# Another cost model and a search in the planner that orders the engines, and other copies in the first head

## The chip, the cores and the metric

The kernel runs on one core of one Trainium2 chip. The metric is the time of one execution on the device in microseconds (us), the median of several runs. Smaller is better.

## The reference

```python
# attention: 2 batches, 8 heads, 768 tokens, 64 values per head
q_bits = (einsum('bhsd,dk->bhsk', q, proj) > 0)        # 6 sign bits of each query; k_bits alike
mask   = q_bucket[:, :, :, None] == k_bucket[:, :, None, :]
scores = where(mask, q @ k.T / sqrt(64), -1e9)
attn   = exp(scores - max(scores)); attn /= sum(attn) + 1e-9
x      = attn @ v                                      # rearranged to 1536 tokens x 512
# first MoE layer, 512 -> 1024 -> 1024 -> 512
x = ((x @ w1) * (x @ w2)) @ w3 @ w_out
# second one, 512 -> 1536 -> 512
out = (sigmoid(x @ w_gate) * (x @ w_val)) @ w_out2
```

The weights come as float64. The kernel keeps them as 64-bit words, converts each 128 x 512 block on the chip, and does the products in float32 halves: an operand is split into a high and a low part, and three matmuls (high-high, high-low, low-high) stand for one product.

## The kernel before

The work has two stages. The first holds the attention, the product of `w3` with `w_out` (`wacc`), and the first MoE layer for the first 512 tokens (`p`, `y`). The second is the function `moe`: 16 tiles of the first layer for the other 1024 tokens and 36 tiles of the second layer. Each of these 52 tiles has 36 matmuls of 512 columns in line 703 (tiles `pa`, `pb`, `m`).

The attention goes over 16 heads with six steps each, a step being 128 queries. A step has four score matmuls of 384 columns (lines 473 and 476), a maximum on VectorE (`sm`, line 482, VectorE is DVE in the profile), an exponential on ScalarE (`e`, line 492, ACT), six 128 x 128 transposes on TensorE (`tp`, line 525, PE), evictions of the transposes by ScalarE and VectorE (`pt`, lines 528 and 530) and six matmuls of 256 columns with the values (`av`, line 543). Each head also has eight hash matmuls of 384 columns (`gps`, lines 393 and 396), with a sign on ScalarE (`sg`) between them. From the second head on, GpSimd (POOL) prepares queries and keys (lines 409 to 411). The first head is made in `first_head` with its own copies: ScalarE rounds the queries and keys to `aq` (line 448), VectorE subtracts this to get `bq` (line 449), GpSimd casts the swapped half twice (`bk`, `ak`, line 453), and ScalarE copies the other half of `bk` (from line 454 on, shown in the trace under the copy helper at line 282). The matrix `pq`, which the hash matmuls read, is written by VectorE at lines 826 and 827 from `pq_raw`, for which ScalarE's queue issues two transfers (lines 434 and 435). The activation table is loaded by an exponential at line 437 that writes into `thr`, the tile that VectorE fills at line 828.

A weight block is loaded into a tile `st` (line 326) and converted by `decode` in six instructions: two on ScalarE (`da`, `dr`, lines 342 and 343), two on GpSimd (`dr`, `da`, lines 344 and 345), a shift on VectorE (`da`, line 346) and a joining operation on VectorE (line 351). 40 of the 76 blocks are converted in the first 345 us.

What sets the order of the first stage is the planner `order_engines`. It is called once, after the first stage's instructions are emitted and before `moe`. It plays the instructions through time with a price for each (`cost`), a delay from engine to engine (`step`), the rings of buffers (`blocked`) and one queue for all transfers. Whenever an engine is free it takes the ready instruction with the lowest `bass_priority`. The order that comes out is pinned, engine by engine, by dependencies that cost no wait between engines. The prices decide nothing on the chip but this order. `moe` is not planned by it.

Of the kernel before, what the change touches and what calls it, by code (L numbers as in the profile page):

```python
# [45 lines left out]
def order_engines(tc):  # L46
# [11 lines left out]
    def count(x):  # L58
        n = 1
        for _, c in list(x.ap)[1:]:  # L60
            n *= c
        return n

    def region(x):

        b = getattr(x, "bass_ap", None)
        if b is None or b.tensor.name not in rings:
            return None
        ap = [list(p) for p in b.ap]
        es = mybir.dt.size(b.dtype)  # L70
        p0, f0 = divmod(b.offset, ap[0][0]) if ap[0][0] else (0, b.offset)
        f1 = f0 + sum((c - 1) * abs(st) for st, c in ap[1:]) + 1
        return b.tensor.name, p0, p0 + ap[0][1], f0 * es, f1 * es

    def cost(k):
        i, e, op = ins[k], eng[k], type(ins[k]).__name__
        rd = [x for x in i.ins if hasattr(x, "ap")]
        n = max([count(i.outs[0])] + [count(x) for x in rd[:1]])
        banks = [x for x in rd + [i.outs[0]] if (region(x) or ("",))[0] in rings and rings[region(x)[0]][0][0] in ("psT", "psS")]
        if e == "PE":  # L80
            passes = 1 if "float32r" in str(rd[0].dtype) else 2 if n == 128 else 4
            return n / 2.4 * passes + (16 if passes == 1 else -12 if passes == 2 else 4)
        if e == "Activation":
            return 971 if n == 768 and banks else 50 + n * (0.836 if banks else 1.0)
        if e == "Pool":
            if op == "InstTensorTensor":
                return 40 + n * 2.4 if n < 768 else 2200
            return 100 + n * 1.15
        if e == "DVE":
            if op == "InstCustomDveAnt":  # L90
                return 720
# [12 lines left out]
    wrote, read, first, uses = {}, {}, {}, {}  # L104
    over = lambda a, b: a[1] < b[2] and b[1] < a[2] and a[3] < b[4] and b[3] < a[4]
    inside = lambda a, b: b[1] <= a[1] and a[2] <= b[2] and b[3] <= a[3] and a[4] <= b[4]
    for k, i in enumerate(ins):
# [26 lines left out]
    left = [len(deps[k]) + len(starts[k]) for k in range(N)]  # L134
# [5 lines left out]
    queue, opens, held, pools = {}, {}, {}, {}  # L140
    for t in sorted(first, key=first.get):
        queue.setdefault(rings[t][0], []).append(t)
        opens.setdefault(first[t], []).append(t)
        pools[rings[t][0][0]] = pools.get(rings[t][0][0], 0) + 1
        for k in uses[t]:
            held.setdefault(k, []).append(t)
    slots = {g: max(rings[t][1] for t in q) for g, q in queue.items()}
    taken = dict.fromkeys(queue, 0)
    todo = {t: len(u) for t, u in uses.items()}

    def blocked(k):
        for t in opens.get(k, ()):
            g = rings[t][0]
            if slots[g] <= 0 or queue[g][taken[g]] != t:
                return g
            if g[0] == "mw" and pools.get("wtmp"):
                return "wtmp"
        return None

    events, ready, waiting = [], {e: [] for e in ranks}, {}  # L160
    at, free, order = [0.0] * N, dict.fromkeys(ranks, 0.0), {e: [] for e in ranks}
    tick = itertools.count()
    dma = 0.0

    def wake(g):
        for k in waiting.pop(g, ()):
            heapq.heappush(ready[eng[k]], (ins[k].bass_priority, k))

    def post(t, what, x):
        heapq.heappush(events, (t, next(tick), what, x))  # L170

    for k in range(N):
        if not left[k]:
            post(0.0, "ready", k)
    while events:
        now = events[0][0]
        while events and events[0][0] <= now:
            _, _, what, x = heapq.heappop(events)
            if what == "ready":
                heapq.heappush(ready[eng[x]], (ins[x].bass_priority, x))  # L180
            elif what == "slot":
                g = rings[x][0]
                slots[g] += 1
                pools[g[0]] -= 1
                wake(g)
                if not pools[g[0]]:
                    wake(g[0])
            elif what == "end":
                for u in ends[x]:
                    left[u] -= 1  # L190
                    at[u] = max(at[u], now + step.get((eng[x], eng[u]), 60))
                    if not left[u]:
                        post(at[u], "ready", u)
                for t in held.get(x, ()):
                    todo[t] -= 1
                    if not todo[t]:
                        post(now + 200, "slot", t)
        again = True
        while again:
            again = False  # L200
            for e in ranks:
                while free[e] <= now and ready[e]:
                    _, k = heapq.heappop(ready[e])
                    g = blocked(k)
                    if g is not None:
                        waiting.setdefault(g, []).append(k)
                        continue
                    for t in opens.get(k, ()):
                        g = rings[t][0]
                        slots[g] -= 1  # L210
                        taken[g] += 1
                        if slots[g] > 0 and waiting.get(g):
                            wake(g)
                            again = True
                    order[e].append(k)
                    for u in begins[k]:
                        left[u] -= 1
                        at[u] = max(at[u], now)
                        if not left[u]:
                            post(at[u], "ready", u)  # L220
                    free[e] = done = now + cost(k)
                    if type(ins[k]).__name__.startswith("InstDMA"):
                        n = count(ins[k].outs[0]) * list(ins[k].outs[0].ap)[0][1] * mybir.dt.size(ins[k].outs[0].dtype)
                        dma = max(now + 1900, dma) + n / 300
                        done = dma + 900
                    post(done, "end", k)
                    post(free[e], "free", k)
# [8 lines left out]
def lsh_attention_moe_moe2_kernel(  # L236
# [57 lines left out]
    pq_raw = cst.tile([P, NB], F32, name="pq_raw")  # L294
# [3 lines left out]
    nthr = cst.tile([P, 1], F32, name="nthr")  # L298
    zb = cst.tile([P, 1], F32, name="zb")
# [129 lines left out]
    def first_head():  # L429
# [525 lines left out]
```

## Time and profile before

| | us |
|---|---|
| median of 3 runs | 812.64 (812.19 to 812.66) |
| the profiled execution's own time | 809.7 |
| its span, first to last instruction | 807.5 |
| TensorE busy | 783.1 (97%) |
| ScalarE busy | 512.4 (63%) |
| VectorE busy | 471.0 (58%) |
| GpSimd busy | 437.0 (54%) |

Times in the trace are microseconds from the start of the span unless marked ns. A busy share of TensorE near 100% doesn't say that it streams at its full rate: its instructions overlap and their ends are modelled, so the spacing of matmuls is the better measure. The chain of work goes back from the last instruction to what released it, step by step, and shows what the time hung on.

### The profile page before, as it was taken

Reading aid. Unit: us, or ns where it says so; the run is one execution under the profiler, and the core shown is the slowest. Engines: PE = TensorE matmul, PEld = TensorE weight load, DVE = VectorE, ACT = ScalarE, POOL = GpSimd, SP = SyncE. Lnnn points to the kernel's source line nnn. Section 1 sums busy time; section 2 is a strip of 40 time slices with the busy share of each in tenths; the row PEclk is TensorE's granted clock in tenths of the full one; section 3 lists DMA queues with packets and bytes.
Section 4 is the critical chain, followed back from the end, with each engine's and each line's share of the span. In section 5 each row is a group of like instructions: output and inputs, shape, how many; then the busy total and the mean of one; then the engine's idle time right before and its main releaser. Section 6 shows DMA issues by size and latency. Waiting matters only on the chain.

```text
span 807.5 us, 11531 instructions
## 1 busy us (share of the span) xinstructions
PE 783.1 (97%) x4016; PEld 657.3 (81%) x4016; DVE 471.0 (58%) x721; ACT 512.4 (63%) x946; POOL 437.0 (54%) x460
## 2 busy tenths in 40 slices
PE   5899999999999999999999999999999999999998
PEld 4787788888888888988888888888888888888886
DVE  5999997775989799773553535655422222222222
ACT  5999997785989888783465556767434333343332
POOL 6778885675576565286355556777523233332320
PEclk9999999999999999999999999999999999999999
DMA  8767676544456574130022123343001000010001
GB/s 263 200 180 184 170 209 170 141 110 109 108 148 167 131 178 118 39 113 0 27 79 78 53 79 105 124 137 105 0 1 53 0 1 1 0 53 1 0 1 52
DMA packets 28584, 74.44 MB, mean 92 GB/s; under 512 B 6128, under 2 KB 8432, under 8 KB 28528
## 3 DMA queue, kind: packets, MB, share of 16 engines
q1 hardware_dynamic: 28368, 73.73, 32.5%
q8 instruction: 31, 0.51, 0.3%
q14 instruction: 25, 0.20, 0.1%
q10 hardware_dynamic: 160, 0.00, 0.0%
HBM read 52.83 MB, written 3.19 MB: 69 GB/s over the span
## 4 chain that ended last, share of the span: by engine, by line
PE 82%; DVE 9%; ACT 3%; POOL 2%; issue 2%; DMA 0%; ACTq 0%; SPq 0%; DVEq 0%; POOLq 0%
PE m L703 18%; PE pa L703 18%; PE pb L703 18%; PE av L543 6%; PE tp L525 5%; PE p L703 5%; PE wacc L598 4%; PE y L703 3%; PE s L476 3%; PE s L473 3%; DVE pt L530 2%; DVE sm L482 2%; PE gps L393 1%; DVE w3f L351 1%; DVE da L346 1%
## 5 line engine op out<-in xcount | busy, mean ns | idle before, releaser
L743 DVE TENSOR_TENSOR pb<-pb,a 128x512 f32<-128x512 f32 x52 | 36.3, 699 | 178.0 <-PE pb L703 173.2
L697 POOL TENSOR_TENSOR wal<-xall,wah 128x512 fp32r<-128x512 f32 x36 | 47.6, 1323 | 107.0 <-ACT wah L282 107.0
L525 PE MATMUL tp<-idf,e 128*128 128x128 f32 x576 | 99.0, 274 | 2.8 <-DVE pt L530 1.5
L482 DVE TENSOR_REDUCE sm<-s 128x1 f32<-128x768 f32 x96 | 90.7, 947 | 17.6 <-PE s L476 17.4
L530 DVE TENSOR_TENSOR pt<-tp,pt 128x512 fp32r<-128x512 f32 x144 | 94.6, 680 | 9.5 <-ACT pt L528 8.7
L703 PE MATMUL pa<-x,wah 128*128 128x512 f32 x320 | 99.8, 391 | 0.0
L703 PE MATMUL pb<-x,wbh 128*128 128x512 f32 x320 | 98.6, 389 | 0.0
L492 ACT ACTIVATE e<-s,sm 128x768 f32<-128x768 f32 x96 | 86.8, 907 | 14.6 <-DVE sm L482 14.4
L344 POOL TENSOR_SCALAR dr<-st 128x512 bf16<-128x512 f32 x76 | 73.8, 981 | 40.8 <-issue 20.8
L528 ACT ACTIVATE pt<-tp 128x512 fp32r<-128x512 f32 x144 | 82.7, 601 | 10.7 <-PE tp L525 9.1
L525 PEld LDWEIGHTS tp<-idf,e 128*128 128x128 f32 x576 | 70.6, 140 | 13.9 <-DVE pt L530 4.3
L543 PE MATMUL av<-pt,spv 128*128 128x256 f32 x576 | 78.9, 286 | 2.8 <-DVE pt L530 2.6
L543 PEld LDWEIGHTS av<-pt,spv 128*128 128x128 f32 x576 | 73.0, 190 | 7.6 <-DVE pt L530 5.7
L703 PEld LDWEIGHTS pa<-x,wah 128*128 128x128 f32 x320 | 60.1, 188 | 13.6
L703 PEld LDWEIGHTS pb<-x,wbh 128*128 128x128 f32 x320 | 60.1, 188 | 12.6
L473 PE MATMUL s<-bk,bq 128*128 128x384 f32 x192 | 61.6, 370 | 4.6 <-ACT e L492 4.5
L598 PE MATMUL wacc<-wo,t 128*128 128x512 f32 x192 | 65.7, 414 | 0.2 <-POOL wo L593 0.2
L345 POOL TENSOR_SCALAR da<-da 128x512 f32<-128x512 f32 x76 | 48.8, 647 | 26.1 <-ACT da L342 22.5
L703 PE MATMUL pa<-x,wal 128*128 128x512 f32 x160 | 62.9, 393 | 0.0
L703 PE MATMUL pb<-x,wbl 128*128 128x512 f32 x160 | 62.3, 389 | 0.0
L476 PE MATMUL s<-ak,aq 128*128 128x384 f32 x192 | 60.3, 368 | 0.3 <-ACT aq L461 0.3
L343 ACT ACTIVATE dr<-st 128x512 int16<-128x512 uint32 x76 | 60.1, 790 | 0.0
(146 smaller groups left out, 1822.1 us busy)
## 6 DMA issues: line engine op xcount, KB each, us to landing
st<-in_moe_w_dram SPq DMA_DIRECT2D x32, 512.0 KB, 4.8
st<-in_moe_w_out_dram SPq DMA_DIRECT2D x20, 512.0 KB, 4.2
st<-in_moe_w_gate_dram SPq DMA_DIRECT2D x12, 512.0 KB, 3.3
st<-in_moe_w_val_dram SPq DMA_DIRECT2D x12, 512.0 KB, 3.2
qk<-in_qk_dram SPq DMA_DIRECT2D x15, 384.0 KB, 4.1
rawv<-in_v_dram SPq DMA_DIRECT2D x16, 192.0 KB, 2.5
rr<-row SPq DMA_DIRECT2D x16, 192.0 KB, 4.1
out_dram<-o SPq DMA_DIRECT2D x12, 256.0 KB, 2.0
```

The costliest lines, as they stand in the source:

```text
L343: act.activation(out=r.bitcast(I16)[:, 0::2], in_=lw, func=AF.Copy, scale=2.0 ** -29)
L344: pool.tensor_scalar(out=r.bitcast(BF16)[:, 1::2], in0=f(hw), scalar1=0.0, scalar2=1.0, op0=ALU.mult, op1=ALU.mult)
L473: pe.matmul(s[:, half, :HS], lhsT=m["bq"][:, qs], rhs=m["bk"][:, ks], start=True, stop=False)
L476: pe.matmul(s[:, half, :HS], lhsT=m["aq"][:, qs], rhs=m["ak"][:, ks], start=False, stop=True)
L482: dve.tensor_reduce(out=b, in_=s[:, :, :HS], op=ALU.max, axis=AX.XY, negate=True)
L492: act.activation(out=e.rearrange("p (a c) -> p a c", a=2), in_=s[:, :, :HS], func=AF.Exp, bias=sm, scale=1.0, accum_out=su_t[h][:, t:t + 1],)
L525: pe.transpose(ps[:, i * P:(i + 1) * P], e_t[g - g % 2 + a][:, c * P:(c + 1) * P], idf)
L528: act.activation(out=dh, in_=src, func=AF.Copy)
L530: dve.tensor_tensor(out=d, in0=src, in1=f(dh), op=ALU.subtract)
L543: pe.matmul(acc[:w.shape[1], :2 * P].rearrange("p (a t) -> p a t", a=2), lhsT=w, rhs=r[:, :, c], start=(c == 0 and i == 0), stop=(c == NT ...
L598: pe.matmul(acc, lhsT=t3[x][:, j], rhs=wo[y][:, j], start=(j == 0 and n == 0), stop=(j == NF1 - 1 and n == 2))
L703: mm = pe.matmul(ps, lhsT=lhs[x], rhs=rhs[y], start=start and n == 0, stop=stop and n == 2)
```

## The change

The planner's function `cost` gets other prices, and marks the instructions of GpSimd and those instructions of VectorE that have at least 128 columns and touch no PSUM. In the plan, a marked instruction of one of the two engines begins only when the last marked one of the other has ended (`lock`). TensorE's matmuls cost double in the plan while `slow` holds, which follows the share of TensorE's time in use. Matmuls of one engine into one PSUM tile keep their program order (`last`). The whole plan is a function `plan(prio)`. It is called once with the priorities as they are, then 400 times with one to eight of them shifted by 50 to 400 from a fixed seed. A trial is kept where the planned end is no later. This happens when the kernel is built; nothing of it runs on the chip.

In the first head, `pq_raw` is loaded once, to 64 partitions, and read for both halves of `pq`. The activation that loads the table writes into a tile of its own, `warm`. Of the copies of the first head's keys, the lower half of `bk` goes from GpSimd to ScalarE, the upper half from ScalarE to VectorE, and `ak` stays on GpSimd.

```diff
+    port = [False] * N
     def cost(k):
...
+        if op.startswith("InstDMA"):
+            return 500
         if e == "PE":
             passes = 1 if "float32r" in str(rd[0].dtype) else 2 if n == 128 else 4
             return n / 2.4 * passes + (16 if passes == 1 else -12 if passes == 2 else 4)
         if e == "Activation":
-            return 971 if n == 768 and banks else 50 + n * (0.836 if banks else 1.0)
+            if banks:
+                return {768: 878, 512: 478, 256: 405}.get(n, 470)
+            return 40 + n + (96 if es == 2 else 0)
         if e == "Pool":
+            port[k] = True
             if op == "InstTensorTensor":
-                return 40 + n * 2.4 if n < 768 else 2200
-            return 100 + n * 1.15
+                return 30 + n * (2.35 if n < 768 else 2.8)
+            return 140 if n < 128 else 715 if es == 2 else 560 if n > 384 else 450
         if e == "DVE":
-            if op == "InstCustomDveAnt":
-                return 720
-            if op in ("InstTensorTensor", "InstTensorReduce") or (op == "InstTensorScalarPtr" and len(rd) > 1 and count(rd[1]) > 8):
-                return 69 + n * (1.04 if banks else 1.4)
-            return 585 if op == "InstTensorScalarPtr" and n == 384 else 69 + n * 0.6
-        return 600
+            two = op in ("InstTensorTensor", "InstCustomDveAnt") or (op == "InstTensorScalarPtr" and len(rd) > 1 and count(rd[1]) > 8)
+            if op == "InstTensorReduce":
+                return 867
+            port[k] = not banks and n >= 128
+            if two and n >= 512:
+                return 600
+            if two:
+                return 85 + n * 1.17 if banks else 60 + n * 1.1
+            return 589 if banks else 60 + n * 0.55
+        return 500
...
+        for w in W:
+            if rings[w[0]][0][0] in ("psT", "psS"):
+                starts[k].update(last.get((e, w[0]), ()))
+                last[e, w[0]] = {k}
...
+    def plan(prio):
...
+                        if port[k]:
+                            begin = max(now, lock["Pool" if e == "DVE" else "DVE"])
+                            lock[e] = begin + c
+                        free[e] = done = begin + c
...
+        return max(free.values()), order
+
+    prio = [i.bass_priority for i in ins]
+    best, order = plan(prio)
+    rng = random.Random(1)
+    for _ in range(400):
+        trial = list(prio)
+        for _ in range(rng.choice((1, 1, 2, 4, 8))):
+            trial[rng.randrange(N)] += rng.choice((-400, -200, -100, -50, 50, 100, 200, 400))
+        span, o = plan(trial)
+        if span <= best:
+            best, order, prio = span, o, trial
...
-    pq_raw = cst.tile([P, NB], F32, name="pq_raw")
+    pq_raw = cst.tile([D, NB], F32, name="pq_raw")
...
+    warm = cst.tile([P, 1], F32, name="warm")
...
-        act.dma_start(out=pq_raw[0:D], in_=proj)
-        act.dma_start(out=pq_raw[D:P], in_=proj)
+        act.dma_start(out=pq_raw, in_=proj)
         dve.memset(zb, -2.0 ** -64)
-        act.activation(out=thr[:, 0:1], in_=zb, func=AF.Exp)
+        act.activation(out=warm, in_=zb, func=AF.Exp)
...
-        for d in ("bk", "ak"):
-            pool.tensor_copy(m[d][0:D], t[1][0:D])
-        act_copy(m["bk"][D:P], f(m["bq"][D:P]))
+        act_copy(m["bk"][0:D], t[1][0:D])
+        dve.tensor_copy(m["bk"][D:P], f(m["bq"][D:P]))
+        pool.tensor_copy(m["ak"][0:D], t[1][0:D])
...
-        dve.tensor_copy(hi, pq_raw[r])
-        dve.tensor_tensor(out=lo, in0=pq_raw[r], in1=f(hi), op=ALU.subtract)
+        dve.tensor_copy(hi, pq_raw)
+        dve.tensor_tensor(out=lo, in0=pq_raw, in1=f(pq[0][0:D, 0:NB]), op=ALU.subtract)
```

## Rows read from the trace of the kernel before

**Rows 1.** The page: busy us per engine, and the granted TensorE clock in 40 slices.

```profile
PE 783.1 (97%) x4016; PEld 657.3 (81%) x4016; DVE 471.0 (58%) x721; ACT 512.4 (63%) x946; POOL 437.0 (54%) x460
...
PEclk9999999999999999999999999999999999999999
```

**Rows 2.** Windows: us, busy (instructions) of PE, PEld, DVE, ACT, POOL, clock, DMA.

```profile
0.00:20.00 20.00, 11.64 (x44) 8.30 (x44) 10.88 (x30) 11.55 (x22) 12.14 (x25) 1.00 0.83 262
20.00:120.00 100.00, 93.60 (x601) 80.32 (x602) 95.37 (x146) 93.96 (x187) 81.21 (x97) 1.00 0.72 190
120.00:180.00 60.00, 57.10 (x339) 49.52 (x338) 45.58 (x67) 46.95 (x91) 38.99 (x48) 1.00 0.53 138
180.00:345.00 165.00, 162.04 (x1038) 144.53 (x1037) 138.71 (x216) 136.31 (x272) 91.28 (x108) 1.00 0.49 125
345.00:807.00 462.00, 458.76 (x2001) 374.60 (x1999) 180.48 (x267) 223.58 (x378) 213.35 (x185) 1.00 0.14 46
```

**Rows 3.** Chain of work in the second stage: start, us, what (one row of many).

```profile
734.85 2.75 PE pa L703 x12
```

**Rows 4.** The same chain where TensorE runs dense in the first stage.

```profile
15.69 1.04 PE gps L393 x6
...
37.19 1.43 PE av L543 x12
```

**Rows 5.** Windows of line 703 alone: us, busy (instructions) of PE and PEld.

```profile
180.00:345.00 165.00, 57.09 (x169) 30.39 (x169) 1.00 0.49 125
```

**Rows 6.** The chain through the first head.

```profile
3.51 0.06 DVE thr L828
...
5.47 0.18 DVE pq L826
...
5.87 2.28 DVE bq L449 x2
8.18 0.84 ACT bk L282
9.04 0.59 ACT sg L395
...
10.40 0.68 DVE ak L459
...
11.74 0.69 PE s L476
...
13.10 0.97 DVE sm L482
```

**Rows 7.** Timeline of the first head, with idle before and what ended it.

```profile
3.51 0.06 DVE L828 MEMSET thr<- 64x1 f32 x1 [2.20 <-ACT thr L437]
...
4.10 1.12 ACT L448 ACTIVATE aq<-qk,scl 128x384 fp32r<-128x384 f32 x2 [0.65 <-DVE scl L834]
...
5.82 0.82 POOL L453 CAST bk<-qk 64x768 fp32r<-64x768 f32 x1 [3.85 <-DMA qk<-in_qk_dram]
...
6.59 1.15 POOL L453 CAST ak<-qk 64x768 fp32r<-64x768 f32 x1
```

**Rows 8.** Line 435 alone: the second transfer of `proj`, issue to landing.

```profile
L435 ACTq DMA_DIRECT2D pq_raw<-in_proj_dram x1: 611/611/611, 1.3 to 1.3; - x1
...
DMA to landing us min/median/max: 4.1/4.1/4.1
```

**Rows 9.** Lines 346 and 351: ns of one, min/median/max; first and last start.

```profile
L346 DVE TENSOR_SCALAR da<-da x76: 378/418/1537, 23.8 to 577.3; 128x512 uint32<-128x512 uint32 x76
...
L351 DVE CUSTOM_DVE_ANT_0 w3f<-da,dr x16: 672/1205/1768, 25.2 to 177.8; 128x1024 uint16<-128x1024 uint16 x16
L351 DVE CUSTOM_DVE_ANT_0 w1r<-da,dr x16: 674/684/876, 201.0 to 544.4; 128x1024 uint16<-128x1024 uint16 x16
```

**Rows 10.** Windows of line 346: us, busy (instructions) of DVE.

```profile
20.00:120.00 100.00, 10.69 (x16) 1.00 0.72 190
```

**Rows 11.** Line 393 in the first 16 us: ns of one, min/median/max.

```profile
L393 PE MATMUL gps<-bq,pq x3: 337/687/688, 7.1 to 15.7; 128*128 128x384 f32 x3
```

More of the change, by code (lines that the diff above doesn't have):

```diff
@@ L2 @@
 import itertools
+import random
 from contextlib import ExitStack, nullcontext
@@ L78, in cost @@
         n = max([count(i.outs[0])] + [count(x) for x in rd[:1]])
-        banks = [x for x in rd + [i.outs[0]] if (region(x) or ("",))[0] in rings and rings[region(x)[0]][0][0] in ("psT", "psS")]
+        bank = lambda x: (region(x) or ("",))[0] in rings and rings[region(x)[0]][0][0] in ("psT", "psS")
+        banks = any(map(bank, rd + [i.outs[0]]))
+        es = mybir.dt.size(i.outs[0].dtype)
+        if op.startswith("InstDMA"):
+            return 500
         if e == "PE":
@@ L103, in order_engines @@
     deps, starts = [set() for _ in ins], [set() for _ in ins]
-    wrote, read, first, uses = {}, {}, {}, {}
+    wrote, read, last, first, uses = {}, {}, {}, {}, {}
     over = lambda a, b: a[1] < b[2] and b[1] < a[2] and a[3] < b[4] and b[3] < a[4]
     inside = lambda a, b: b[1] <= a[1] and a[2] <= b[2] and b[3] <= a[3] and a[4] <= b[4]
-    for k, i in enumerate(ins):
+    for k, (i, e) in enumerate(zip(ins, eng)):
         R = [r for r in map(region, i.ins) if r]
@@ L133, in order_engines @@
     ends, begins = [[] for _ in ins], [[] for _ in ins]
-    left = [len(deps[k]) + len(starts[k]) for k in range(N)]
     for k in range(N):
@@ L139, in order_engines @@
             begins[j].append(k)
-    queue, opens, held, pools = {}, {}, {}, {}
+    queue, opens, held, pools0 = {}, {}, {}, {}
     for t in sorted(first, key=first.get):
@@ L143, in order_engines @@
         opens.setdefault(first[t], []).append(t)
-        pools[rings[t][0][0]] = pools.get(rings[t][0][0], 0) + 1
+        pools0[rings[t][0][0]] = pools0.get(rings[t][0][0], 0) + 1
         for k in uses[t]:
             held.setdefault(k, []).append(t)
[L147 to L216, printed above, removed]
@@ new lines, in order_engines, with blocked, wake, post @@
+    WINDOW = 3413.0
+    costs = [cost(k) for k in range(N)]
+    left0 = [len(deps[k]) + len(starts[k]) for k in range(N)]
+    loads = [type(i).__name__.startswith("InstDMA") for i in ins]
+    def plan(prio):
+        left, pools, todo = list(left0), dict(pools0), {t: len(u) for t, u in uses.items()}
+        slots = {g: max(rings[t][1] for t in q) for g, q in queue.items()}
+        taken = dict.fromkeys(queue, 0)
+        def blocked(k):
+            for t in opens.get(k, ()):
+                g = rings[t][0]
+                if slots[g] <= 0 or queue[g][taken[g]] != t:
+                    return g
+                if g[0] == "mw" and pools.get("wtmp"):
+                    return "wtmp"
+            return None
+        events, ready, waiting = [], {e: [] for e in ranks}, {}
+        at, free, order = [0.0] * N, dict.fromkeys(ranks, 0.0), {e: [] for e in ranks}
+        tick = itertools.count()
+        dma = 0.0
+        slow, window, used, spill = True, 0, 0.0, 0.0
+        lock = {"DVE": 0.0, "Pool": 0.0}
+        def wake(g):
+            for k in waiting.pop(g, ()):
+                heapq.heappush(ready[eng[k]], (prio[k], k))
+        def post(t, what, x):
+            heapq.heappush(events, (t, next(tick), what, x))
+        for k in range(N):
+            if not left[k]:
+                post(0.0, "ready", k)
+        while events:
+            now = events[0][0]
+            while events and events[0][0] <= now:
+                _, _, what, x = heapq.heappop(events)
+                if what == "ready":
+                    heapq.heappush(ready[eng[x]], (prio[x], x))
+                elif what == "slot":
+                    g = rings[x][0]
+                    slots[g] += 1
+                    pools[g[0]] -= 1
+                    wake(g)
+                    if not pools[g[0]]:
+                        wake(g[0])
+                elif what == "end":
+                    for u in ends[x]:
@@ L217, in order_engines @@
                         left[u] -= 1
-                        at[u] = max(at[u], now)
+                        at[u] = max(at[u], now + step.get((eng[x], eng[u]), 60))
                         if not left[u]:
                             post(at[u], "ready", u)
[L221 to L225, printed above, removed]
@@ L226, in order_engines @@
-                    post(done, "end", k)
-                    post(free[e], "free", k)
+                    for t in held.get(x, ()):
+                        todo[t] -= 1
+                        if not todo[t]:
+                            post(now + 200, "slot", t)
+            again = True
+            while again:
+                again = False
+                for e in ranks:
+                    while free[e] <= now and ready[e]:
+                        _, k = heapq.heappop(ready[e])
+                        g = blocked(k)
+                        if g is not None:
+                            waiting.setdefault(g, []).append(k)
+                            continue
+                        for t in opens.get(k, ()):
+                            g = rings[t][0]
+                            slots[g] -= 1
+                            taken[g] += 1
+                            if slots[g] > 0 and waiting.get(g):
+                                wake(g)
+                                again = True
+                        order[e].append(k)
+                        for u in begins[k]:
+                            left[u] -= 1
+                            at[u] = max(at[u], now)
+                            if not left[u]:
+                                post(at[u], "ready", u)
+                        begin, c = now, costs[k]
+                        if e == "PE":
+                            while (window + 1) * WINDOW <= now:
+                                share, window, used = used / WINDOW, window + 1, spill
+                                spill = 0.0
+                                slow = share <= 0.75 if slow else share < 0.45
+                            c *= 2 if slow else 1
+                            inside = min(c, (window + 1) * WINDOW - now)
+                            used, spill = used + inside, spill + c - inside
+                        if port[k]:
+                            begin = max(now, lock["Pool" if e == "DVE" else "DVE"])
+                            lock[e] = begin + c
+                        free[e] = done = begin + c
+                        if loads[k]:
+                            n = count(ins[k].outs[0]) * list(ins[k].outs[0].ap)[0][1] * mybir.dt.size(ins[k].outs[0].dtype)
+                            dma = max(now + 1900, dma) + n / 300
+                            done = dma + 900
+                        post(done, "end", k)
+                        post(free[e], "free", k)
@@ new lines, in plan @@
+        if sum(map(len, order.values())) != N:
+            return float("inf"), order
+        return max(free.values()), order
[9 more added lines that the diff above has]
+            best, order, prio = span, o, trial
```

## The prediction

> **What bounds the kernel now.** I read the page first, then the busy times by stage, then the chain of work. The page [rows 1] gives TensorE 97% busy, so the question is where it streams and where it only looks busy. In the second stage the chain is TensorE alone: twelve matmuls of line 703 in 2.75 us, 229 ns each [rows 3]. The 52 tiles of `moe` have 1872 of them, 429 us, more than half of the span, and the planner doesn't touch them. The last row of the stages [rows 2] agrees: from 345 us to the last matmul at some 804 there is no hole.
>
> The first 345 us are another matter. The code gives the matmuls: 576 transposes, 576 of 256 columns, 384 scores, 128 hashes and 192 for `wacc`; line 703 adds 169 by then [rows 5]. The planner prices them 95, 123, 176, 176 and 229 ns, and dense stretches agree: six hashes in 1.04 us, twelve of `av` in 1.43 [rows 4]. The sum is 54.7 + 70.8 + 67.6 + 22.5 + 44.0 + 38.7 = 298 us, so some 47 us of the 345 are lost to TensorE. In the first 20 us only 44 matmuls run [rows 2], at most 44 x 176 ns = 7.7 us of work, so 12 us or more are lost there; the other 35 or so lie between 20 and 345.
>
> Why they are lost: from 20 to 120 us VectorE is busy 95.4 of 100 us and ScalarE 94.0, while TensorE's busy time has holes [rows 2]. There VectorE sets the pace. From 120 to 345 no engine beside TensorE is full (VectorE 45.6 of 60 and 138.7 of 165), and what is lost is short waits between the four engines of the attention.
>
> **The first head.** Here the chain [rows 6] is a list of single steps, and the change cuts four of them.
> - VectorE waits 2.20 us until the table's activation has written `thr` [rows 7], because both write one tile. With `warm` its small fills end near 2.0 us instead of 4.07, and `aq`, which waited 0.65 us for them, starts with ScalarE free at 3.5 instead of 4.10.
> - The second transfer of `proj` lands at 1.31 + 4.1 = 5.4 us [rows 8], and the second `pq` copy starts at 5.47 [rows 6]. It goes. The first transfer was issued 0.57 us earlier and the first copy ran at 5.08, behind other VectorE work. So `pq` is ready somewhere between 3.5 and 5.1; I take 4.1.
> - `bq` starts at 5.87 and its two halves take 2.28 us [rows 6]. All that time GpSimd casts `bk` and `ak` (5.82 to 7.74) [rows 7]. The same kind of subtraction, 512 columns out of SBUF, isn't in these rows, but the joining operation with two SBUF inputs takes 0.67 us where it is undisturbed and 1.2 in the median where GpSimd is at work [rows 9]; three quarters of 0.67 is 0.5. In the new order `bq` can run from 4.2 to 5.2, before the swapped keys land at 5.8 and GpSimd starts at all. It ends at 5.2 instead of 8.15.
> - ScalarE's copy of `bk` (0.84 us) stands ahead of `sg` on ScalarE [rows 6]. It goes to VectorE, where nothing waits behind it but `ak` at the end of the hash chain. In its place ScalarE casts the lower half, 5.8 to some 6.65, since it too waits for the swapped keys. So `sg` starts between 5.9 (ahead of that cast) and 6.65 (behind it) instead of 9.04: a lead of 2.4 to 3.1 us.
>
> The rest of the head (hash, `ak`, score, maximum) has the same links as before, so the first maximum moves from 13.1 to some 10.5. I take 2.6 us. The bounds are 0.5, if `bq` still meets GpSimd's cast because the planner puts VectorE's other work ahead, and 3.1. From the first maximums on VectorE has hardly a pause until 120 us [rows 2], and after 180 TensorE has hardly one, so a lead at the start is passed on to the end: the cover for it is the lack of any timed event later on, except landings of transfers. If weight blocks were late, the lead would be eaten; their queue is 0.83 busy in the first 20 us [rows 2], so that isn't excluded.
>
> [...]
>
> **The planner.** Its prices move towards the spacing seen in the trace where VectorE is full. The shift went from 376 to 342 and the joining operation from 720 to 600. The trace has 378 and 672 as their shortest busy time [rows 9], which includes some 60 to 80 ns that overlap the next instruction (the maximum is busy 0.97 us in the chain [rows 6] and priced 867). So the prices are now right for undisturbed instructions. What disturbs them is priced apart, by the exclusion, and the trace has it: the shift takes 378 ns at best and 1537 at worst, and joining `w3f` takes 1205 in the median against 684 for `w1r` [rows 9]. Between 20 and 120 us sixteen shifts take 10.69 us, 668 ns each [rows 10]; undisturbed they would take 6.0. Sixteen joinings lose up to 0.5 us each, 8 us. So 8 to 12 us of VectorE's 95 there are waits for GpSimd. [...]
>
> What an order can get back of this is bounded by two things. GpSimd is itself busy 81 of 100 us in that stage [rows 2], so most shifts will meet some GpSimd instruction in any order. And the plan takes the first ready instruction; it doesn't look for a free slot, so only the 400 trials bring the waits down. I take a quarter to a third of 8 to 12 us: 3 us. For 120 to 345, where some 18 us are lost in short waits, I take a tenth, 2 us, for an order that was searched on a closer timeline. Both ends are far: if all 35 us between 20 and 345 went, the gain would be 35; and since another order can also place blocks worse, it may be a loss of some 7 (below).
>
> Sum: 2.6 + 3 + 2 = 7.6, say 8 us. Of the profiled execution's 809.7 us this leaves 801.7. The median of the runs is 2.9 us above that execution, so 804.6. No instruction is added to the second stage, and at its end nothing moves.
>
> **The rivals.**
> - Only the head counts. The plan's timeline is off by more than the slots it saves, and the order comes out different but no better: 812.6 - 2.6 = 810.0. For it speaks that a wait is decided by which engine issues first, by tenths of a microsecond (the same shift takes 378 or 1537 ns [rows 9]). [...]
> - The blocks come too early: slower. Joining is 120 ns cheaper in the plan and the shift 34, so it may place more weight blocks before 120 us. There VectorE has 4.6 us free [rows 2]. A block costs it 0.42 + 0.68 = 1.1 us alone and 0.67 + 1.2 = 1.9 us against GpSimd [rows 9, 10]. From about three more blocks than now it pushes the attention. With six more, 6 x 1.9 - 4.6 = 6.8 us, less the head's 2.6: 4.2 us slower, 816.8. Against it: the attention's priorities are lower numbers in the same steps, and the exclusion makes blocks dearer, not cheaper, where GpSimd is busy.
> [...]
> - Much more: the closer model frees most of VectorE's waits and shortens the waits after 120 us, 15 us or more: 797 or less. TensorE's 47 us leave room for it.
>
> **How the numbers follow.** Forecast, 799 to 808.5: 0.45. Only the head, to 810.9: 0.15. Much more: 0.10. Nothing arrives: 0.12. Blocks too early, or another order that is worse by more than the head brings: 0.18. Likeliest 804.6. The range leaves out the further half of the last and about half of the big gain: 796 to 815. A measurement of this kernel tells about 0.2%, 1.6 us, from no change. Faster by more: 0.45 + 0.15 + 0.10 = 0.70. Within: 0.12. Slower: 0.18.
>
> **What would show it.** In the changed kernel's trace: VectorE's fills without the wait of 2.2 us; `bq` at some 0.5 us each and done near 5.2; the first maximum near 10.5; the mean of the shift between 20 and 120 us under 668 ns; VectorE's busy time for the same work in this stage lower; the first `pa` matmul of `moe`, and so the last matmul, some 8 us earlier; and the second stage at 2.75 us per twelve matmuls as before. The prediction is wrong if the first maximum is early and the end isn't, or if more than some 19 shifts stand before 120 us.

## The result, and the profile after

The changed kernel takes 803.8 us (median of five, 802.7 to 806.8) against 812.3 before: a ratio of 0.991, 95% interval 0.989 to 0.993. 804.6 was forecast, with 796 to 815 as the range.

The page of the changed kernel, busy times per engine (line numbers are some 50 higher than before: line 482 is 535, 346 is 400, 703 is 756):

```profile
span 805.0 us, 11532 instructions
...
PE 781.3 (97%) x4016; PEld 661.1 (82%) x4016; DVE 470.9 (59%) x722; ACT 511.4 (64%) x946; POOL 434.2 (54%) x459
```

No engine's work got less than that of [rows 1] by more than 3 us. What changed is when it is done. This trace is of the longest of the five executions (806.8 us), and the trace of before is of one below its median (809.7), so the two spans are only 2.5 us apart. The changed kernel was therefore profiled a second time (`e4_repeat` below, 803.4 us). The stages of both, in the columns of [rows 2]; first the changed kernel, then its second trace from 20 to 180 us, with the stage up to 120 us in two parts:

```profile
0.00:20.00 20.00, 12.18 (x44) 9.85 (x44) 12.20 (x34) 13.72 (x24) 13.25 (x26) 1.00 0.91 278
20.00:120.00 100.00, 92.73 (x599) 82.42 (x600) 93.34 (x142) 91.55 (x184) 76.92 (x94) 0.98 0.72 184
120.00:180.00 60.00, 59.30 (x363) 52.97 (x362) 48.42 (x70) 46.99 (x93) 38.73 (x48) 1.00 0.52 147
180.00:345.00 165.00, 160.86 (x1038) 144.91 (x1037) 136.13 (x215) 137.66 (x274) 96.89 (x111) 1.00 0.47 128
```

```profile
20.00:60.00 40.00, 35.77 (x239) 31.56 (x240) 38.34 (x59) 36.01 (x75) 27.02 (x36) 1.00 0.79 192
60.00:120.00 60.00, 57.24 (x376) 51.39 (x375) 56.32 (x87) 56.62 (x114) 51.18 (x62) 1.00 0.71 184
120.00:180.00 60.00, 59.30 (x364) 53.04 (x363) 48.43 (x70) 46.50 (x92) 37.91 (x47) 1.00 0.54 147
```

Before, TensorE had 355 matmuls between 60 and 120 us:

```profile
60.00:120.00 60.00, 56.76 (x355) 47.73 (x355) 55.68 (x84) 55.95 (x110) 51.10 (x62) 1.00 0.72 187
```

Now it has 376, and 364 instead of 339 between 120 and 180 [rows 2]. Most of the time comes from there. To compare traces I price each matmul as the prediction did (95, 123, 176 and 229 ns by kind) and subtract the sum from the time gone by. This is what TensorE has lost, in us, by the end of each stage (one trace each; the last three rows are kernels of the experiments below):

| kernel | by 20 | by 60 | by 120 | by 180 | by 345 |
|---|---|---|---|---|---|
| before | 13.2 | 20.7 | 30.3 | 36.5 | 47.9 |
| changed | 13.2 | 24.0 | 30.3 | 33.0 | 43.4 |
| changed, second trace | 13.2 | 22.0 | 28.2 | 31.0 | 40.0 |
| planner alone | 14.4 | 22.5 | 30.5 | 32.9 | 40.9 |
| without the exclusion | 13.2 | 20.9 | 31.7 | 35.9 | 50.1 |
| old model, searched | 12.4 | 20.2 | 30.7 | 34.5 | 48.8 |

In the second trace 8 us less are lost by 345 us: 6.8 less between 60 and 180 and 2.4 less after that, against 1.3 more before 60. The first `pa` matmul of `moe`, at 353.0 us before, comes at 348.7 and 345.1. The changed kernel first, then the second trace:

```profile
348.68 0.63 PE L756 MATMUL pa<-x,wah 128*128 128x512 f32 x2
```

```profile
345.13 0.63 PE L756 MATMUL pa<-x,wah 128*128 128x512 f32 x2
```

The end doesn't move by as much. From that matmul to the end of the span it is 454.4 us before and 456.3 in both traces of the changed kernel, so the second stage gives back 1.9 us. Between 400 and 600 us TensorE runs seven matmuls fewer, though the profile shows it busy throughout at full clock. Before, then the planner alone (with the first head of before), then the second trace (us, busy and matmuls, granted clock, transfers):

```profile
400.00:600.00 200.00, 200.00 (x871) 1.00 0.24 79
```

```profile
400.00:600.00 200.00, 200.00 (x871) 1.00 0.24 77
```

```profile
400.00:600.00 200.00, 200.00 (x864) 1.00 0.23 77
```

At 229 ns these seven are 1.6 us; from 600 to 780 us the three kernels run 786 each. All twelve traces with the new first head have 863 or 864 there, the two with the old one have 871. So it comes with the head's edits, although none of their instructions runs in this stretch. Why is open; no run takes these edits apart.

The first trace has 2 us more of loss by 60 us, and the granted clock shows where. These are windows of TensorE in the first trace (us, busy and matmuls, granted clock, transfers), then the same windows in the second:

```profile
44.00:48.00 4.00, 2.84 (x10) 0.90 0.52 108
48.00:52.00 4.00, 4.00 (x22) 0.67 0.86 270
```

```profile
44.00:48.00 4.00, 3.10 (x15) 1.00 0.63 130
48.00:52.00 4.00, 4.00 (x34) 1.00 1.00 319
```

The order is the same in both, and TensorE has a thin stretch at 44 to 48 us in both (10 and 15 matmuls). Only in the first did its granted clock then fall, to 0.50 from 48 to 50 us:

```profile
48.00:50.00 2.00, 2.00 (x8) 0.50 0.96 264
```

From 48 to 52 us 22 matmuls ran there, at a mean granted clock of 0.67, and 34 in the second trace, at 1.00.

The first head, in the changed kernel's timeline:

```profile
1.28 0.06 DVE L881 MEMSET thr<- 64x1 f32 x1
...
3.37 1.12 ACT L501 ACTIVATE aq<-qk,scl 128x384 fp32r<-128x384 f32 x2 [0.56 <-DMA qk<-in_qk_dram]
...
4.83 1.71 DVE L502 SCALAR_TENSOR_TENSOR bq<-qk,scl,aq 128x384 fp32r<-128x384 f32 x2
...
5.30 0.83 POOL L507 CAST ak<-qk 64x768 fp32r<-64x768 f32 x1 [3.34 <-DMA qk<-in_qk_dram]
...
11.30 1.82 DVE L535 TENSOR_REDUCE sm<-s 128x1 f32<-128x768 f32 x2 [1.01 <-PE s L529]
```

The fill of `thr` no longer waits, `aq` waits for its data only, and the first maximum comes at 11.3 us instead of 13.1 [rows 6].

### The profile page after: what moved, and what is told of

Its sections match the earlier page's. It is cut to its first block, busy times and chain, and to the rows that moved or that the text cites. A ratio compares the mean times of both kernels' runs of the same rounds, so it can differ in the third digit from the quotient of the medians.

```text
span 805.0 us, 11532 instructions
## 1 busy us (share of the span) xinstructions
PE 781.3 (97%) x4016; PEld 661.1 (82%) x4016; DVE 470.9 (59%) x722; ACT 511.4 (64%) x946; POOL 434.2 (54%) x459
## 4 chain that ended last, share of the span: by engine, by line
PE 84%; ACT 7%; POOL 3%; DVE 2%; issue 2%; DMA 2%; SPq 0%; ACTq 0%; POOLq 0%; DVEq 0%
PE m L756 18%; PE pa L756 18%; PE pb L756 18%; PE av L596 6%; PE tp L578 5%; PE p L756 5%; PE wacc L651 4%; PE s L526 3%; PE s L529 3%; PE y L756 2%; ACT e L545 2%; ACT pt L581 2%; PE gps L447 2%; DMA st<-in_moe_w_dram 1%; DVE sm L535 1%
## 5 line engine op out<-in xcount | busy, mean ns | idle before, releaser
L578 PE MATMUL tp<-idf,e 128*128 128x128 f32 x576 | 95.8, 274 | 4.8 <-ACT e L545 2.3
L545 ACT ACTIVATE e<-s,sm 128x768 f32<-128x768 f32 x96 | 86.7, 906 | 10.5 <-DVE sm L535 8.5
L578 PEld LDWEIGHTS tp<-idf,e 128*128 128x128 f32 x576 | 71.7, 141 | 15.7 <-ACT e L545 3.4
L651 PE MATMUL wacc<-wo,t 128*128 128x512 f32 x192 | 61.9, 410 | 1.2 <-POOL wo L646 0.9
```

The source lines that it names most:

```text
L545: act.activation(out=e.rearrange("p (a c) -> p a c", a=2), in_=s[:, :, :HS], func=AF.Exp, bias=sm, scale=1.0, accum_out=su_t[h][:, t:t + 1],)
L578: pe.transpose(ps[:, i * P:(i + 1) * P], e_t[g - g % 2 + a][:, c * P:(c + 1) * P], idf)
L651: pe.matmul(acc, lhsT=t3[x][:, j], rhs=wo[y][:, j], start=(j == 0 and n == 0), stop=(j == NF1 - 1 and n == 2))
```

## The experiments

Each was timed beside the kernel before on the same chip (811.7 to 811.8 us there).

**The head alone.** The planner of before, the edits of the first head.

```diff
+        act_copy(m["bk"][0:D], t[1][0:D])
+        dve.tensor_copy(m["bk"][D:P], f(m["bq"][D:P]))
...
 (planner as before)
```

> The first head's edits alone, with the planner of the kernel before. The prediction's sum gives the head 2.6 us and the planner 5, so 809.7 to 810.5 with a first maximum near 11.3 us, as in the changed kernel's trace (13.1 before). Rival, the head is everything: 804, as the whole change. Rival, the head's lead is eaten because the order was planned for other instructions: 812 to 813.

Measured: 811.6 us, ratio 1.000 (0.999 to 1.002). The first maximum is at 10.4 us, 2.7 earlier, and nothing is left of it at the end, as in the rival where the lead is eaten.

**The planner alone.** The other half.

```diff
+    port = [False] * N
...
+    def plan(prio):
...
 (first head as before)
```

> The new planner alone (prices, exclusion, clock, 400 trials), with the first head as before. By the sum: 812.3 less 6 to 7, 805.5 to 806.5. If the head is everything: 812. If head and order only work together, both this and the head alone stay above 810.

Measured: 805.0 us, 0.993 (0.990 to 0.995). So the planner carries the change: 6.8 us, with a first head that stays as it was.

**No trials.**

```diff
-    for _ in range(400):
+    for _ in range(0):
```

> The whole change without the 400 trials: the new prices, exclusion and clock plan once. By the prediction only the trials bring the waits for GpSimd down, so this should lose 2 to 4 us against the changed kernel: 806 to 808. Rival, the closer prices alone do it: 804. Rival, the new prices alone make a worse order, which the trials mend: 811 or more.

Measured: 814.0 us, 1.003 (1.002 to 1.004), slower than before. The new prices, the exclusion and the clock rule alone order worse; the trials bring 9 us. Windows of this kernel, then what TensorE waited for in the same stretch (engine, line, releaser: us, times, longest):

```profile
60.00:120.00 60.00, 54.27 (x339) 47.48 (x338) 50.13 (x77) 51.02 (x101) 43.91 (x52) 0.97 0.67 178
```

```profile
PE s L526 <- ACT e L545: 3.7, 3, 1.8
```

The second trace of the changed kernel has 376 matmuls in this stretch and 1.3 us of this wait:

```profile
PE s L526 <- ACT e L545: 1.3, 2, 0.7
```

VectorE is busy 50.1 us here and 56.3 there. The trials didn't take work away from VectorE; they kept it fed. The granted clock isn't what makes the 9 us: the two executions of this kernel at a mean clock of 1.000 took 811.2 and 813.0 us.

**The changed kernel once more.**

```diff
 (nothing changed)
```

> The changed kernel once more, unchanged, for its time beside the others and for a second trace. 803 to 805. The first trace shows the granted clock at half from 47 to 51 us, and its execution took 806.8. If that fall comes in some executions only, this trace may be without it and end some 2 to 4 us earlier; if it comes in each, it is here too, at the same place.

Measured: 805.1 us, 0.992 (0.990 to 0.993). The trace has no fall of the clock in the first stage; it stands above. Over the eleven timed executions of the changed kernel, those with a mean clock of 0.999 or 1.000 took 802.2 to 803.8 us, those with 0.995 to 0.998 took 804.8 to 806.8. So the fall is not in each execution, and the change would be worth some 2 us more without it.

**Without the exclusion.**

```diff
-                        if port[k]:
+                        if False:
```

> The changed kernel with the plan's exclusion of VectorE and GpSimd taken out; prices, clock rule and 400 trials kept. If the exclusion is what makes the trials worth 9 us, this is at 811 or more. If it is worth only what the lock waits are, 3 us by the prediction: 806 to 808. If the trials' gain doesn't come from the exclusion: 803 to 805.5.

Measured: 811.4 us, 1.000 (0.998 to 1.001). The whole gain is gone, at full clock too (808.1 to 811.7 in the four executions at 1.000).

**Without the clock rule.**

```diff
-                            c *= 2 if slow else 1
+                            c *= 1
```

> The changed kernel with matmuls in the plan always at the full clock; prices, exclusion and trials kept. If the clock rule is what gives the trials something that the chip also feels (thin stretches of TensorE), this is at 811 or more. If the exclusion does it: 803 to 806. The timed executions of the changed kernel themselves differ by at most some 4 us with the granted clock, so the falls of the clock alone can't be worth 9.

Measured: 808.1 us, 0.996 (0.994 to 0.998): between the two expectations. Some 3 to 4 us of the gain hang on it. Its executions also spread widely, from 805.2 at a clock of 1.000 to 813.4 at 0.992.

**Another seed.**

```diff
-    rng = random.Random(1)
+    rng = random.Random(2)
```

> The changed kernel with another seed for its 400 trials. If the trials find what the model tells them, this is within 3 us of it: 802 to 808. If the changed kernel's seed was a lucky draw, this is back at 810 to 815.

Measured: 805.5 us, 0.992 (0.989 to 0.994). So the first seed was no lucky draw.

**The old model, searched.** Old prices, no exclusion, no clock rule, with the new head and 400 trials.

```diff
 (prices of before)
-                        if port[k]:
+                        if False:
...
-                            c *= 2 if slow else 1
+                            c *= 1
```

> The new first head and the 400 trials, but with the prices of before and neither exclusion nor clock rule. If any search does it, because it packs a timeline however rough: 804 to 806. If the model is what counts: 810 to 813, as the head alone (811.6).

Measured: 811.8 us, 1.000 (0.999 to 1.001). This search in a rough model brought nothing. Together: the trials need the model (811.8 with them in the old one) and the model needs the trials (814.0 without).

**The head with the order of before written out.**

```diff
     assert sum(map(len, order.values())) == N, "the list schedule is stuck"
+    order = {"PE": [40, 45, 41, ...], ...}    # the order of the kernel before, edited instructions put in or left out
```

> The first head's edits with the order of the kernel before written out, engine by engine (only the edited instructions are put in or left out), so that the head is the only thing that differs. The head alone under the old planner made the first maximum 2.7 us earlier and won nothing (811.6), with 171 of TensorE's 2144 places moved by more than two. If that small new order cost the lead: 809 to 810. If waits that don't move with the head (transfers that land when they land, VectorE) take the lead back: 811 to 812.5.

Measured: 809.4 us, 0.997 (0.996 to 0.998), a gain of 2.3 us. So the head brings nearly what was forecast, though its second stage has the loss told above, and the head alone had lost it to a small new order. The two traces show how. The head alone: VectorE's reciprocal of the sums, then the row's transfers in the SP queue, GpSimd's scaling that waits for the row, and windows of TensorE:

```profile
47.19 0.17 DVE L504 RECIPROCAL rs<-su 128x6 f32<-128x6 f32 x1
```

```profile
48.49 0.62 SPq L423 DMA_DIRECT2D bq<-aq  x1
49.16 0.58 SPq L506 DMA_DIRECT2D row<-rs  x1
...
55.96 0.47 SPq L510 DMA_DIRECT2D rr<-row  x1
```

```profile
56.83 0.51 POOL L411 CAST aq<-qk 128x384 fp32r<-128x384 f32 x1
59.73 2.21 POOL L515 TENSOR_TENSOR xall<-xall,rr 128x768 f32<-128x768 f32 x1 [2.39 <-DVE pt L530]
```

```profile
60.00:64.00 4.00, 1.90 (x9) 0.92 0.00 0
64.00:68.00 4.00, 4.00 (x21) 0.65 0.85 189
```

With the order of before, the same reciprocal, queue, engine and window:

```profile
44.91 0.19 DVE L511 RECIPROCAL rs<-su 128x6 f32<-128x6 f32 x1
```

```profile
45.67 0.89 SPq L513 DMA_DIRECT2D row<-rs  x1
...
51.50 0.46 SPq L517 DMA_DIRECT2D rr<-row  x1
```

```profile
57.22 2.25 POOL L522 TENSOR_TENSOR xall<-xall,rr 128x768 f32<-128x768 f32 x1
```

```profile
60.00:64.00 4.00, 3.90 (x22) 1.00 0.23 48
```

With the planner's new order the reciprocal comes 2.3 us later (47.19 against 44.91). Then the row of sums stands in the SP queue behind three transfers of the next head's keys and queries and goes 1.8 us after it is ready. It takes 6.8 us to land, against 3.5 with the old order, and its second half goes right after that, 4.5 us later than with the old order. GpSimd takes the scaling in between two steps of the next head (the cast to `aq` and the subtraction to `bq`) and stands still for 2.4 us. The profile names a VectorE instruction, but the second transfer, issued at 55.96 and landed 3.6 us later, is what came last. TensorE waits 2.1 us for that `bq`, runs 9 matmuls in four microseconds instead of 22, and its clock falls right after. The three executions of the head alone at a clock of 1.000 took 810.5 to 812.6 us, no less than those at 0.998 and 0.999 (809.7 to 812.1); only the two at 0.997 are longer (814.7 and 814.9). So the fall alone doesn't explain the lost lead. That the late row does is read from this pair of traces; no run moves the row alone.

**The old prices.** Exclusion, clock rule and trials kept.

```diff
-            if two and n >= 512:
-                return 600
+            if op == "InstCustomDveAnt":
+                return 720
...
 (the rest of the prices as before)
```

> The changed kernel with the old price list; exclusion, clock rule and 400 trials kept. Without the exclusion the gain was gone (811.4), without the clock rule it was 808.1. If the finer prices matter as well: 808 to 811. If the exclusion and the clock rule carry it all: 803.5 to 806.

Measured: 810.7 us, 0.999 (0.997 to 1.000), at the far end of what was expected if the prices matter. None of its twelve executions has a full clock (0.993 to 0.998); those at 0.997 and 0.998 took 808.6 to 809.8 us.

Each of the kernels that lack a piece is one order from one seed. The whole model was searched with two seeds, once with the old head and once with later landings (the last experiment), and gave 803.8 to 805.5 us each time. But with 3000 trials, next, it gave 810.0, about as much as those that lack a piece. So how much of each loss is the missing piece and how much the draw of the order isn't shown; a second seed for these kernels would have told.

**3000 trials.**

```diff
-    for _ in range(400):
+    for _ in range(3000):
```

> The changed kernel with 3000 trials instead of 400. If what the plan gains beyond 400 trials reaches the chip: 801 to 803.5, faster than the changed kernel. If the plan is by then fitted to its own errors: 804 to 807.

Measured: 810.0 us, 0.997 (0.995 to 0.999), 6 us slower than with 400. In its trace, the window of 80 to 90 us, and the wait that ended in it:

```profile
80.00:90.00 10.00, 7.42 (x32) 6.82 (x32) 4.17 (x7) 3.46 (x7) 4.47 (x5) 0.66 0.79 191
```

```profile
82.58 0.98 PE L526 MATMUL s<-bk,bq 128*128 128x384 f32 x2 [4.32 <-DMA rawv<-in_v_dram]
```

The profile names a transfer of `v`, but a score matmul doesn't read `v`, and that transfer landed 7.2 us after its issue at 78.50, when TensorE was running again. What the matmul reads is `bq`. The last transfer into it, and its size and time to landing:

```profile
73.09 0.55 SPq L476 DMA_DIRECT2D bq<-aq  x1
```

```profile
bq<-aq SPq DMA_DIRECT2D x1, 192.0 KB, 9.2
```

So it landed at some 82.3 us, right before the matmul. Issued ahead of it, from 68.98 on, were two weight blocks that took 8.9 us:

```profile
st<-in_moe_w_dram SPq DMA_DIRECT2D x2, 512.0 KB, 8.9
```

TensorE stands still for 4.3 us behind this half of the next head's queries, the other engines stand still behind TensorE (between 80 and 90 us none of them is busy for half of the time), and the clock falls. None of the twelve executions has a full clock (0.993 to 0.998); the two at 0.998 took 804.1 and 807.5 us. I read this as an order that the further trials moved into a gap that the plan has and the chip doesn't; the next run bears on it.

**3000 trials with later landings.** Transfers from a tile on the chip end 1.2 us later in the plan.

```diff
-                            done = dma + 900
+                            done = dma + (2100 if region(ins[k].ins[0]) else 900)
```

> As the one with 3000 trials, but transfers from a tile on the chip (rows of sums, halves of keys) land 1.2 us later in the plan: 4.0 us from the free queue for the 3 KB row, whose median from issue to landing is 3.5 to 4.3 us in the traces. If a late row or half that holds up GpSimd's queue is part of what is left: 799 to 802. If not, the same as with 3000 trials.

Measured: 804.2 us, 0.991 (0.989 to 0.994): no better than 400 trials, but 6 us better than 3000 without it. It fits the reading that the longer search had used up landings that the plan prices too short, and the transfers that it makes later are of the kind that TensorE waited for at 82 us. Since it is one draw of another order, it doesn't show it. None of these kernels beats the changed one clearly.

## Why the prediction was right

**The number.** 804.6 was forecast and 803.8 measured (805.1 when it was timed once more), but the sum came out partly by luck. Set the second trace of the changed kernel against before, with the table. The head's 2.6 us had gone by 20 us, where both have lost 13.2. Between 20 and 120 us 2.1 us came back, and none in the first trace, where 3 were forecast. Between 120 and 345 it was 5.8 us (4.5 in the first trace) where 2 were forecast. After that 1.9 us were lost where none were. One term was too small and the others too large.

**The bound.** Right for the first stage: TensorE lost 47 us in the first 345, and the gain came out of these. For the second stage the prediction said that no instruction is added to it, and so put it at nothing. None was added, and it still gave back 1.9 us, with the head's edits.

**The head.** 2.6 us were forecast; by itself, with the rest of the order held, it is 2.3. In the changed kernel the steps came out as listed, but for two. `pq`, `bits` and `pat` stand ahead of `bq` on VectorE, so `bq` starts at 4.83, not 4.2. And the swapped keys landed before 5.3, not at 5.8, so its second half did meet GpSimd's cast: 1.71 us for both, not 1.0. That makes 1.8 us at the first maximum, and none by 20 us (the table). The new order converts a first weight block in this stretch: its shift starts at 15.1 us in the second trace, where before the first one starts at 23.8 [rows 9], and its joining, at 16.19, stands in the chain of work ahead of the next maximum. The planner alone (805.0) is as fast as the whole change (805.1, timed beside it): it has lost 0.9 us more by 345, and 0.9 less after the first `pa` matmul (455.4 us to the end against 456.3). So the sentence that a lead at the start is passed on to the end holds only while the order behind it is the same. The planner makes a new one for every edit, and what that costs or brings is as large as the head.

**The planner.** 5 us were forecast, 6.8 measured without the head's edits. That only the trials would bring it was right, and more so than written: without them the change is slower than before. The step that failed is the place of the gain. The prediction took 3 us from fewer waits of VectorE for GpSimd between 20 and 120 us. The shift in that stretch in the changed kernel, then the joining operation, before and in the changed kernel:

```profile
20.00:120.00 100.00, 10.05 (x15) 0.98 0.72 184
```

```profile
20.00:120.00 100.00, 15.63 (x16) 1.00 0.72 190
```

```profile
20.00:120.00 100.00, 13.88 (x15) 0.98 0.72 184
```

The shift takes 670 ns each, against 668 [rows 10], and the joining 925 against 977. From 120 to 345 us the joining is longer instead (930 ns against 898). Over 20 to 345 us the two together take 1.54 us a block, against 1.55 before and 1.57 without the exclusion, so the 40 blocks make little more than 1 us of difference. Nor is VectorE's busy time for the same work lower: 93.3 us for 142 instructions between 20 and 120 us, 95.4 for 146 before. The waits for GpSimd are about as long as before. And still nothing is gained without the exclusion in the plan. So it doesn't act mainly by avoiding these waits.

What it does act by is open. The reading that I can offer: with it in the plan, the times at which VectorE's and GpSimd's results are ready are closer to the chip's, and an order that was searched on them keeps the loop of score, maximum, exponential and transpose fed. Between 120 and 180 us VectorE's wait for scores falls from 8.1 us in nine waits to 4.5 in eight; before, the second trace, then without the exclusion and the old model:

```profile
DVE sm L482 <- PE s L476: 8.1, 9, 1.7
```

```profile
DVE sm L535 <- PE s L529: 4.5, 8, 1.3
```

```profile
DVE sm L535 <- PE s L529: 4.0, 4, 1.9
```

```profile
DVE sm L524 <- PE s L518: 5.8, 6, 2.0
```

But it falls without the exclusion as well, and TensorE loses less there than before in all searched kernels of the table (2.4 to 4.2 us against 6.2). The two without the exclusion lose their gain elsewhere: 10.8 and 10.5 us between 60 and 120, where before it was 9.6 and the changed kernel loses 6.3 and 6.2, and 14.2 and 14.3 us between 180 and 345, where before it was 11.4 and the changed kernel loses 10.4 and 9.0. So the wait for scores doesn't tell a kernel that gains from one that doesn't.

The second part of the forecast was sized at 2 us for all of 120 to 345; the table shows 3.4 between 120 and 180 alone. That the truer timeline is the reason is argued from the four kernels that lack a piece of it or all (811.4, 808.1, 810.7, 811.8) and are slower, each a single order; no run measured how far a plan lies from the chip, instruction by instruction. Nor does a run part the two things that the exclusion does in the plan: it says when VectorE and GpSimd wait, and it makes their instructions longer.

**The rivals.** Blocks too early didn't come: 15 shifts between 20 and 120 us and one before, sixteen as ever. The rival that only the head counts fell with the planner alone. What it rested on, a plan that is off by more than it saves, is a possible reason of what 3000 trials lost; it isn't shown.

**The clock.** Before, the same hash matmul takes 687 ns at the start and 337 at 15.7 us [rows 11]. In the first trace of the changed kernel hash matmuls are still 0.32 us apart from 13.9 to 15.2 us; in the second they are 0.17 apart from 13.6 to 14.3. The granted clock reads 1.00 up to 20 us in both, and both have lost 13.2 us by then, so the slower spacing isn't what took the lead. A fall of the granted clock came later and elsewhere, after a thin stretch at 44 to 48 us, in some executions.

## What to carry to other kernels

A planner's order can be searched, and here the search paid only in a model whose prices and exclusions were taken from the trace: the kernels that lacked one of the three pieces were 3 to 8 us slower (one order each), the search in the old model gave nothing, and the model without the search was slower than before. Test such an order on the chip with two seeds and with fewer and more trials, since the longer search was the slower one here. To measure an edit in a planned kernel, hold the rest of the order fixed; otherwise the new plan is measured with it. And look at the stages that an edit doesn't touch: here one of them got 1.9 us longer. Where the profile names the last releaser of a wait, check that the instruction reads what that releaser wrote.

## What the runs showed of the hardware

The same program with the same order has its TensorE clock fall in some executions and not in others: a mean granted clock of 0.995 to 1.000 in the changed kernel, over 4 us in time, and 0.992 to 1.000 without the clock rule, over 8 us. The kernel before stayed at 0.999 or 1.000 in 77 of the 80 executions that were timed beside the experiments; the other three, at 0.995 to 0.998, took 813.5 to 814.4 us. In the changed kernel the fall came after a thin stretch at 44 to 48 us (10 matmuls, 2.84 us busy), where before TensorE runs 25 and is busy throughout. The thin stretch is there without a fall too (15 matmuls, 3.10 us busy), and what decides between the two isn't shown.

A transfer issued behind large ones landed late: with 3000 trials 192 KB issued after two weight blocks took 9.2 us to land. In the changed kernel the 15 transfers of this kind took 2.5 to 8.1 us, 5.0 in the median.

VectorE's shift and joining took longer before where they began while GpSimd was at work. A shift that began 0.04 us after GpSimd's subtraction of line 593 took 1.54 us and ended 0.29 us after it; one that began 0.26 us before the same subtraction took 0.43:

```profile
70.97 0.69 DVE L530 TENSOR_TENSOR pt<-tp,pt 128x512 fp32r<-128x512 f32 x1
...
71.54 1.29 POOL L593 TENSOR_TENSOR wo<-wor,wo 128x512 fp32r<-128x512 f32 x1
...
71.58 1.54 DVE L346 TENSOR_SCALAR da<-da 128x512 uint32<-128x512 uint32 x1
...
73.04 0.94 DVE L482 TENSOR_REDUCE sm<-s 128x1 f32<-128x768 f32 x1
```

```profile
88.64 0.43 DVE L346 TENSOR_SCALAR da<-da 128x512 uint32<-128x512 uint32 x1
...
88.90 1.31 POOL L593 TENSOR_TENSOR wo<-wor,wo 128x512 fp32r<-128x512 f32 x1 [1.22 <-ACT wo L282]
```

Of the 40 joinings up to 345 us in that trace, the 18 that began within an instruction of GpSimd took 0.67 to 1.77 us, 1.17 in the median; the 22 others took 0.67 to 0.69. The rows at 70.97 to 73.04 us also show what a busy time of VectorE includes: each of the first two runs 0.08 us into the next.

The spacing of matmuls can change with edits far away from them. Between 400 and 600 us, with TensorE busy throughout in the profile and its granted clock full, 871 matmuls run with the old first head and 863 or 864 with the new one. The cause isn't known.
